# First weights of a fused attention and Mish layer joined from 16-bit halves, and differences moved from GpSimd to VectorE between the two stages

## The chip, the core and the metric

The kernel runs on one core of a Trainium2 chip. The metric is the device time of one execution in microseconds (us); the kernel before took 827.08 us (median of 3 runs, 826.86 to 828.69). The engines are TensorE (PE in the rows; PEld is its weight load), VectorE (DVE), ScalarE (ACT), GpSimd (POOL) and the queue engine SyncE (SP), which issues most transfers.

## What is computed

An attention with queries averaged in pairs, then a two-layer feed-forward block with the Mish function:

```python
q_pool = q.reshape(B, H, S // 2, 2, D).mean(axis=3)            # B, H, S, D = 4, 8, 1152, 64
scores = np.matmul(q_pool, k.transpose(0, 1, 3, 2)) / sqrt(D)
attn = softmax(scores)                                          # over 1152 keys
x = (attn @ v) laid out as 2304 tokens x 512
h = x @ w_in                                                    # 512 x 2048
out = (h * tanh(softplus(h))) @ w_out                           # 2048 x 512
```

q, k and v are float32; w_in and w_out come as float64 and have to be made float32 on the chip.

## The kernel before

**Attention.** 32 steps, one for each batch, pair of heads and half of the 576 queries. A step `i` has nine chunks `c` of 128 keys for both heads of the pair. In the names of the plan: QK(i, c) is TensorE's scores into PSUM; CP copies them to SBUF on ScalarE; MX and MXF keep running maxima on VectorE; MT, TMAX and MB (TensorE, VectorE, TensorE) bring the maximum over keys to every partition; SUB (VectorE) and EXP (ScalarE) work in four groups of chunks; ADD(i, 0 to 4) sums the exponentials on GpSimd, where ADD(i, 2) is a transfer that GpSimd issues and that adds in flight; PV is the product with v; PVE copies it out; FIN0 sums over partitions on TensorE. The division is done by FLN, FEX, FC, FE, FT, FU, FX on ScalarE and GpSimd, and for the last two steps by LX(i) on VectorE (an addition, a reciprocal, a product). The result is xT, x transposed.

**Feed-forward.** x and the weights go into TensorE as a high part (fp32r) and a rest, three products for each. split_h(u, c) rounds a piece of x (unit u of 256 tokens, quarter c of 512) on ScalarE, and split_l(u, c) takes the difference that is the rest; H_(u, f) is the first layer for a unit and a slice of 128 hidden columns; A_g and A_gh are Mish in full and rounded; D_gl is their difference on VectorE; O_(u, f) is the second layer, and EV takes it out of PSUM, for the first block on ScalarE. split_l runs on GpSimd, but for units 5 to 8 in quarters 2 and 3 on VectorE.

**Weights.** 32 pieces of 128 x 512; load_w(n) is the transfer of the raw 64-bit numbers, conv(n, m) the conversion: m = 0 rescales the high word on ScalarE, m = 1, 2 and 3 are three VectorE instructions that shift the exponent into place, put in the sign, and put in three bits of the low word; m = 4 rounds the high part on ScalarE, and m = 5 takes the rest by a difference on GpSimd. Pieces 0 to 3 are converted in steps 0 to 4 of the attention (m = 0 into PSUM there), pieces 4 to 8 in the border between the stages.

**What sets the order.** Each engine runs its instructions in program order, and waits on semaphores. The program order is a sort by planned times in units of a step: FILL lists the first steps one by one, STEP gives each later step, END overrides the last steps (NS = 32), TAIL lists the border with the first units of the feed-forward, FLOW the rest.

Of the kernel before, what the change touches and what calls it, by code (L numbers as in the profile page):

```python
# [22 lines left out]
def tile_pooled_attention_then_mish_ffn(ctx: ExitStack, tc: tile.TileContext, q, k, v, moe_w_in, moe_w_out, out):  # L23
# [43 lines left out]
    if True:  # L67
# [352 lines left out]
        FILL = [  # L420
            (-0.891, load_q, 0, 0),
            (-0.802, load_k, 0, (0, 2)),
            (-0.762, load_k, 0, (2, 5)),
            (-0.703, load_k, 0, (5, 9)),
            (-0.643, QH, 0),
            (-0.624, load_w, 0),
            (-0.602, QK, 0, 0),
            (-0.506, QK, 0, 1),
            (-0.486, CP, 0, 0),
            (-0.466, load_q, 0, 1),  # L430
            (-0.427, QK, 0, 2),
            (-0.407, CP, 0, 1),
            (-0.377, load_w, 1),
            (-0.351, MX, 0, 1),
            (-0.348, QK, 0, 3),
            (-0.328, CP, 0, 2),
            (-0.286, conv, 0, 0),
            (-0.269, QK, 0, 4),
            (-0.253, MX, 0, 3),
            (-0.219, load_k, 1),  # L440
            (-0.218, QH, 1),
            (-0.209, QK, 0, 5),
            (-0.192, MX, 0, 4),
            (-0.187, CP, 0, 3),
            (-0.138, MX, 0, 5),
            (-0.131, QK, 0, 6),
            (-0.084, conv, 0, 1),
            (-0.073, CP, 0, 5),
            (-0.070, QK, 0, 7),
            (-0.041, load_q, 1),  # L450
            (-0.035, MX, 0, 6),
            (-0.016, QK, 1, 0),
            (0.019, MX, 0, 7),
            (0.030, CP, 0, 6),
            (0.073, conv, 0, 2),
            (0.084, CP, 0, 7),
            (0.087, QK, 0, 8),
            (0.137, load_v, 0),
            (0.137, conv, 0, 3),
            (0.154, CP, 0, 8),  # L460
            (0.197, conv, 1, 0),
            (0.210, MX, 0, 8),
            (0.236, CP, 1, 0),
            (0.264, conv, 1, 1),
            (0.279, conv, 0, 4),
            (0.293, QK, 1, 1),
            (0.295, QP, 1),
            (0.313, MXF, 0),
            (0.315, load_w, 2),
            (0.367, MX, 1, 1),  # L470
            (0.379, MT, 0),
            (0.414, conv, 0, 5),
            (0.421, conv, 1, 2),
            (0.427, QK, 1, 2),
            (0.432, CP, 1, 1),
            (0.470, TMAX, 0),
            (0.487, CP, 1, 2),
            (0.489, QK, 1, 3),
            (0.530, conv, 1, 3),
            (0.543, QK, 1, 4),  # L480
            (0.578, MX, 1, 3),
            (0.591, MB, 0),
            (0.594, load_w, 3),
            (0.632, MX, 1, 4),
            (0.644, CP, 1, 3),
            (0.686, conv, 2, 0),
            (0.686, SUB, 0, 1),
            (0.700, QK, 1, 5),
            (0.725, CP, 1, 4),
            (0.752, load_q, 2),  # L490
            (0.768, CP, 1, 5),
            (0.782, QK, 1, 6),
            (0.789, SUB, 0, 0),
            (0.810, EXP, 0, 1),
            (0.892, MX, 1, 5),
            (0.902, EXP, 0, 0),
            (0.946, SUB, 0, 2),
            (0.958, QK, 1, 7),
            (0.989, CP, 1, 6),
            (1.008, ADD, 0, 0),  # L500
            (1.014, PV, 0, 0),
            (1.031, CP, 1, 7),
            (1.049, MX, 1, 6),
# [4 lines left out]
            (1.157, SUB, 0, 3),
            (1.169, QK, 1, 8),
            (1.225, PV, 0, 2),  # L510
            (1.228, ADD, 0, 1),
            (1.237, CP, 1, 8),
            (1.238, load_k, 2),
            (1.268, PV, 0, 1),
            (1.279, CP, 2, 0),
            (1.308, MX, 1, 8),
            (1.335, QK, 2, 1),
            (1.362, conv, 2, 1),
            (1.391, PV, 0, 5),
            (1.403, CP, 2, 1),  # L520
            (1.411, MXF, 1),
            (1.416, load_v, 1),
            (1.435, PV, 0, 4),
            (1.446, EXP, 0, 3),
            (1.465, MX, 2, 1),
            (1.482, MT, 1),
            (1.519, conv, 2, 2),
            (1.531, QK, 2, 2),
            (1.568, TMAX, 1),
            (1.570, QK, 2, 3),  # L530
            (1.590, ADD, 0, 2),
            (1.590, CP, 2, 2),
            (1.627, MX, 2, 3),
            (1.632, conv, 1, 4),
            (1.639, MB, 1),
            (1.674, QK, 2, 4),
            (1.690, SUB, 1, 0),
            (1.691, conv, 1, 5),
            (1.693, CP, 2, 3),
            (1.721, PV, 0, 6),  # L540
            (1.735, CP, 2, 4),
            (1.765, PV, 0, 7),
            (1.793, MX, 2, 4),
            (1.804, EXP, 1, 0),
            (1.812, QK, 2, 5),
            (1.847, SUB, 1, 1),
            (1.860, QK, 2, 6),
            (1.890, CP, 2, 5),
            (1.916, PV, 0, 8),
            (1.933, CP, 2, 6),  # L550
            (1.950, MX, 2, 5),
            (1.975, EXP, 1, 1),
            (2.004, MX, 2, 6),
            (2.016, QK, 2, 7),
            (2.058, SUB, 1, 2),
            (2.070, QK, 2, 8),
            (2.081, ADD, 1, 0),
            (2.084, CP, 2, 7),
            (2.126, PVE, 0),
            (2.150, CP, 2, 8),  # L560
            (2.161, MX, 2, 7),
            (2.163, PV, 1, 3),
            (2.215, MX, 2, 8),
            (2.227, QK, 3, 0),
            (2.269, conv, 2, 3),
            (2.283, PV, 1, 0),
            (2.301, ADD, 0, 3),
            (2.318, MXF, 2),
# [1000 lines left out]
```

## Time and profile before

| | |
|---|---|
| profiled execution | 827.53 us, span 825.5 us |
| median of 3 runs | 827.08 us |
| TensorE busy | 802.4 us, 97% of the span |
| VectorE, ScalarE, GpSimd busy | 566.4, 507.2 and 400.9 us |
| granted TensorE clock, mean | 0.99 |
| attention | up to about 419 us, a step 12.3 us |

A row of the timeline has the start in us, the length, the engine, the line, the operation, out<-in with shapes, how many instructions are merged, and in brackets the idle time of the engine before it with what ended it. Busy shares are means over stages with different limits, so the stages have to be read one by one.

### The profile page before, as it was taken

The page shows a single profiled execution, that of the slowest core. Times are in us where ns is not written, and L with a number is a line of the kernel's source. Part 1 is how long each engine was busy: PE and PEld are TensorE (multiplying, and loading weights), DVE is VectorE, ACT ScalarE, POOL GpSimd, SP SyncE. Part 2 cuts the span into 40 slices and gives each one's busy share as a digit, 9 for nine tenths or more (in the row PEclk, how much of TensorE's full clock was granted, in tenths as well). Part 3 has the DMA queues.
Part 4 walks back from the last instruction along what each step waited for, and adds up shares of the span by engine and source line. Part 5 has one row for each costly group of instructions (what it writes and reads, how often), then busy time and mean ns, then how long its engine had stood idle before and what let it go on. Part 6 is the DMA issues. An engine that isn't in the chain of part 4 may idle for free.

```text
span 825.5 us, 12804 instructions
## 1 busy us (share of the span) xinstructions
PE 802.4 (97%) x4979; PEld 543.1 (66%) x4979; DVE 566.4 (69%) x690; ACT 507.2 (61%) x864; POOL 400.9 (49%) x332
## 2 busy tenths in 40 slices
PE   7899999999999999999998999999999999999997
PEld 4354554554555555554577888888888888888886
DVE  6999999999999999999947334545654433432222
ACT  5799999999999999998956622232333233212211
POOL 2479998898898898897985101110120111100000
PEclk9999999999999999999998999999999999999999
DMA  6446467556557656555422101111120111001111
GB/s 236 138 131 146 120 152 173 138 135 152 126 142 173 144 174 145 130 123 116 87 44 77 52 26 51 52 52 42 60 77 26 52 51 52 1 26 51 52 45 57
DMA packets 21515, 78.93 MB, mean 96 GB/s; under 512 B 2128, under 2 KB 6992, under 8 KB 21456
## 3 DMA queue, kind: packets, MB, share of 16 engines
q0 software_dynamic: 4608, 28.31, 19.2%
q1 hardware_dynamic: 16848, 49.81, 16.5%
q8 instruction: 39, 0.64, 0.3%
q14 instruction: 20, 0.16, 0.1%
HBM read 45.09 MB, written 4.72 MB: 60 GB/s over the span
## 4 chain that ended last, share of the span: by engine, by line
PE 81%; DVE 5%; POOL 5%; ACT 4%; DMA 3%; issue 2%; DVEq 0%; POOLq 0%; ACTq 0%
PE h L1034 22%; PE s L156 18%; PE pv L238 14%; PE o L1075 10%; DMA acc<-TB 3%; PE Sb L260 2%; POOL acc L230 2%; PE mt L192 2%; DVE rmax L177 1%; DVE TA L215 1%; ACT TA L166 1%; POOL acc L224 1%; PE Mb L209 1%; POOL acc L226 1%; ACT TA L219 1%
## 5 line engine op out<-in xcount | busy, mean ns | idle before, releaser
L156 PE MATMUL s<-qT,kT 64*128 64x288 f32 x1152 | 204.4, 451 | 8.9 <-ACT TA L166 3.5
L1043 ACT ACTIVATE g<-h 128x512 f32<-128x512 f32 (+1 forms) x88 | 45.7, 523 | 251.4 <-PE h L1034 251.4
L1051 DVE TENSOR_TENSOR gl<-g,gh 128x512 fp32r<-128x512 f32 (+1 forms) x88 | 55.9, 638 | 201.9 <-ACT gh L1047 196.6
L156 PEld LDWEIGHTS s<-qT,kT 64*128 64x128 f32 x1152 | 93.0, 187 | 105.9 <-DVE rmax L177 27.0
L418 POOL TENSOR_TENSOR wl<-wt,wh 128x512 fp32r<-128x512 f32 x32 | 44.3, 1385 | 242.9 <-ACT wh L415 189.3
L166 ACT COPY TA<-s 128x576 f32<-128x576 f32 x192 | 117.6, 638 | 25.5 <-PE s L156 16.8
L215 DVE TENSOR_TENSOR TA<-TA,Mb 128x1152 f32<-128x1152 f32 x96 | 129.1, 1349 | 2.0 <-PE Mb L209 0.7
L1034 PE MATMUL h<-xh,wh 128*128 128x512 f32 (+1 forms) x352 | 124.7, 354 | 0.0
L1034 PE MATMUL h<-xl,wh 128*128 128x512 f32 (+1 forms) x352 | 124.1, 353 | 0.1
L1034 PE MATMUL h<-xh,wl 128*128 128x512 f32 (+1 forms) x352 | 124.1, 353 | 0.0
L238 PE MATMUL pv<-TA,vn 128*64 128x288 f32 x768 | 115.5, 421 | 0.4 <-ACT pvs L249 0.4
L219 ACT ACTIVATE TA<-TA 128x1152 f32<-128x1152 f32 x96 | 112.8, 1175 | 2.9 <-DVE TA L215 2.3
L224 POOL TENSOR_TENSOR acc<-TA 128x1152 f32<-128x1152 f32 x32 | 85.0, 2657 | 45.3 <-ACT TA L219 29.8
L230 POOL TENSOR_TENSOR acc<-acc 128x576 f32<-128x576 f32 x64 | 91.2, 1425 | 9.3 <-DMA acc<-TB 7.8
L177 DVE TENSOR_TENSOR rmax<-s,rmax 128x576 f32<-128x576 f32 x128 | 93.7, 752 | 1.3 <-ACT TB L166 0.7
L238 PEld LDWEIGHTS pv<-TA,vn 128*64 128x64 f32 x768 | 47.1, 137 | 47.7 <-issue 10.1
L1034 PEld LDWEIGHTS h<-xh,wh 128*128 128x128 f32 x352 | 66.8, 190 | 10.8 <-issue 0.4
L1034 PEld LDWEIGHTS h<-xl,wh 128*128 128x128 f32 x352 | 66.8, 190 | 10.2 <-DVE xl L1006 0.3
L1034 PEld LDWEIGHTS h<-xh,wl 128*128 128x128 f32 x352 | 66.9, 190 | 9.4
L215 DVE TENSOR_TENSOR TB<-TB,Mb 128x1728 f32<-128x1728 f32 x32 | 62.2, 1945 | 0.0
L166 ACT COPY TB<-s 128x576 f32<-128x576 f32 x96 | 59.4, 651 | 4.2 <-PE s L156 3.3
L238 PE MATMUL pv<-TB,vn 128*64 128x288 f32 x384 | 61.5, 415 | 0.2
(404 smaller groups left out, 1326.8 us busy)
## 6 DMA issues: line engine op xcount, KB each, us to landing
acc<-TB POOLq DMA_DIRECT2D x32, 864.0 KB, 7.2
vn<-in_v_dram SPq DMA_DIRECT2D x16, 576.0 KB, 6.3
kT<-in_k_dram SPq DMA_DIRECT2D x15, 576.0 KB, 5.3
qn<-in_q_dram SPq DMA_DIRECT2D x15, 576.0 KB, 6.3
ri<-in_moe_w_in_dram SPq DMA_DIRECT2D x16, 512.0 KB, 3.3
ro<-in_moe_w_out_dram SPq DMA_DIRECT2D x16, 512.0 KB, 3.3
out_dram<-xT SPq DMA_DIRECT2D x18, 256.0 KB, 2.6
qn<-in_q_dram SPq DMA_DIRECT2D x2, 288.0 KB, 4.5
```

The source lines that it names most:

```text
L156: pe.matmul(s[:, j, 0:HQ], kT[64 * j:64 * j + 64, c], qT[64 * j:64 * j + 64, hf], start=True, stop=True,)
L166: act.copy(T(i, c), ss[i, c])
L177: dve.tensor_tensor(ss[i, c] if c == FOLD else r, ss[i, c], x, ALU.max)
L215: dve.tensor_tensor(x, x, Mbs[i].unsqueeze(1).to_broadcast([P, w, W]), ALU.subtract)
L219: act.activation(x, x, AF.Exp, scale=0.0625)
L224: pool.tensor_tensor(accs[i][:, 0:2], T(i, 0, 2), T(i, 2, 4), ALU.add)
L230: pool.tensor_tensor(accs[i][:, 0], accs[i][:, 0], accs[i][:, n - 2], ALU.add)
L238: pe.matmul(pvs[i][64 * j:64 * j + 64, 0:HQ], vn[:, j, c, :], T(i, c)[:, j], start=(pvn[i] == 1), stop=(pvn[i] == NC),)
L1034: pe.matmul(o, a, b, start=(m == 0), stop=(m == len(seq) - 1))
L1043: act.activation(ch[bu, f], hs[bu, f], AF.Mish)
L1051: dve.tensor_tensor(gl, ch.pop((bu, f)), f32(gs[bu, f][0]), ALU.subtract)
L1075: pe.matmul(os_[bu][t], x, y, start=(first and m == 0), stop=(last and m == 2))
```

## The change

For pieces 0 to 3 the float32 word is put together from 16-bit halves: a ScalarE instruction writes the three low bits as an unsigned 16-bit number into the lower half, a GpSimd instruction writes the sign (0 or 32768) into the upper half, and one VectorE instruction shifts the rescaled exponent and mantissa from PSUM and joins them. In the border, split_l of units 5, 6 and 7 is on VectorE in all quarters, and that of unit 8 on GpSimd; conv(n, 5) is on VectorE for pieces 4 to 8. FILL, END, TAIL and two planned times have new numbers; the set of steps is the same.

```diff
+U16 = mybir.dt.uint16
...
+            if n not in wt:
+                wt[n] = wraw_p.tile([P, DM], F32, tag="wt", name=f"wt{n}")
+            if n < 4 and 0 < m < 4:
+                z = wt[n].bitcast(U16).rearrange("p (m two) -> p m two", two=2)
+                u = x.bitcast(U16)
+                if m == 1:
+                    act.activation(z[:, :, 0], u[:, :, 1], AF.Copy, bias=2.0**-14 - 0.5, scale=2.0**-13)
+                elif m == 2:
+                    pool.tensor_scalar(z[:, :, 1], u[:, :, 3], 32768.0, 32768.0, ALU.is_ge, ALU.mult)
+                else:
+                    w = wt[n].bitcast(I32)
+                    dve.scalar_tensor_tensor(
+                        w, in0=cw[n].bitcast(I32), scalar=3, in1=w, op0=ALU.logical_shift_left, op1=ALU.bitwise_or
+                    )
+                return
             if m == 0:
-                wt[n] = wraw_p.tile([P, DM], F32, tag="wt", name=f"wt{n}")
...
-                pool.tensor_tensor(lo, wt[n], f32(hi), ALU.subtract)
+                (dve if 3 < n < 9 else pool).tensor_tensor(lo, wt[n], f32(hi), ALU.subtract)
...
-            e = dve if u > 4 and c in XD else pool
+            e = dve if 4 < u < 8 and c in XD else pool
...
-        XD, ED = (2, 3), ()
+        XD, ED = (0, 1, 2, 3), ()
...
-            (-0.2644, split_h, 3, 3),
+            (-3.3977, conv, 4, 0),
```

How this moves instructions is shown at three places. First VectorE in step 0, from the maximum of chunk 5 to the TMAX of step 0 (s are scores, rmax the running maxima, cw and wt a piece in work, m the maximum). Before:

```order
L177 TENSOR_TENSOR rmax0_0_153<-s0_5_170,rmax0_0_153 128x576
L400 TENSOR_SCALAR cw0_160<-cw0_160 128x512
L177 TENSOR_TENSOR rmax0_1_173<-s0_6_177,rmax0_1_173 128x576
L177 TENSOR_TENSOR rmax0_0_153<-s0_7_183,rmax0_0_153 128x576
L402 SCALAR_TENSOR_TENSOR cw0_160<-ri0_137,cw0_160 128x512
L406 SCALAR_TENSOR_TENSOR wt0_159<-ri0_137,cw0_160 128x512
L177 TENSOR_TENSOR s0_8_196<-s0_8_196,rmax0_1_173 128x2x288
L400 TENSOR_SCALAR cw1_204<-cw1_204 128x512
L181 TENSOR_TENSOR rmax0_0_153<-s0_8_196,rmax0_0_153 128x576
L177 TENSOR_TENSOR rmax1_0_219<-s1_1_212,TA3_101 128x576
L402 SCALAR_TENSOR_TENSOR cw1_204<-ri1_151,cw1_204 128x512
L198 TENSOR_REDUCE m0_238<-mt0_221 128x5
```

and now:

```order
L178 TENSOR_TENSOR rmax0_0_153<-s0_5_171,rmax0_0_153 128x576
L178 TENSOR_TENSOR rmax0_1_174<-s0_6_179,rmax0_1_174 128x576
L405 SCALAR_TENSOR_TENSOR wt0_159<-cw0_161,wt0_159 128x512
L178 TENSOR_TENSOR rmax0_0_153<-s0_7_185,rmax0_0_153 128x576
L178 TENSOR_TENSOR s0_8_196<-s0_8_196,rmax0_1_174 128x2x288
L182 TENSOR_TENSOR rmax0_0_153<-s0_8_196,rmax0_0_153 128x576
L178 TENSOR_TENSOR rmax1_0_216<-s1_1_204,TA3_101 128x576
L199 TENSOR_REDUCE m0_234<-mt0_220 128x5
```

Of the five conversion instructions in this stretch one is left; piece 1 has none before step 2.

Then GpSimd from the affine select at the start to the transfer ADD(0, 2) (qT is the pair sum of queries, wl the rest of a piece, acc the sum of exponentials). Before:

```order
L133 TENSOR_TENSOR qT0_109<-qn0_131 128x288
L130 TENSOR_TENSOR qT1_166<-qn1_186 128x576
L418 TENSOR_TENSOR wl0_0_210<-wt0_159,wh0_0_209 128x512
L224 TENSOR_TENSOR acc0_287<-TA3_101 128x1152
L226 TENSOR_TENSOR acc0_287<-TA3_101 128x576
L228 DMA acc0_287<-TB3_102 128x1728
```

and now:

```order
L402 TENSOR_SCALAR wt0_159<-ri0_137 128x512
L134 TENSOR_TENSOR qT0_109<-qn0_131 128x288
L131 TENSOR_TENSOR qT1_167<-qn1_188 128x576
L433 TENSOR_TENSOR wl0_0_213<-wt0_159,wh0_0_212 128x512
L225 TENSOR_TENSOR acc0_281<-TA3_101 128x1152
L402 TENSOR_SCALAR wt1_209<-ri1_151 128x512
L227 TENSOR_TENSOR acc0_281<-TA3_101 128x576
L433 TENSOR_TENSOR wl0_1_344<-wt1_209,wh0_1_343 128x512
L402 TENSOR_SCALAR wt3_380<-ro1_339 128x512
L402 TENSOR_SCALAR wt2_332<-ro0_218 128x512
L229 DMA acc0_281<-TB3_102 128x1728
```

The four sign instructions (L402) stand ahead of the second half of the first queries, of ADD(0, 1), and, the last two with one difference, of the transfer.

Last GpSimd in the border, from ADD(31, 3) and ADD(31, 4) on (es, pvs and rs belong to the division of step 29, xl is the rest of x). Before:

```order
L230 TENSOR_TENSOR acc31_4033<-acc31_4033 128x576 x2
L276 TENSOR_TENSOR es29_4050<-es29_4050,rs29_4068 128x288
L1006 TENSOR_TENSOR xl2_3961<-xT_60,xh2_3960 128x256
L291 TENSOR_TENSOR pvs29_3901<-pvs29_3901,rs29_4068 128x288
L295 TENSOR_TENSOR xT_60<-es29_4050,pvs29_3901 128x288
L1006 TENSOR_TENSOR xl2_3961<-xT_60,xh2_3960 128x256 x3
L1006 TENSOR_TENSOR xl3_4249<-xT_60,xh3_4248 128x256
L418 TENSOR_TENSOR wl0_2_4295<-wt4_3985,wh0_2_4294 128x512
L1006 TENSOR_TENSOR xl3_4249<-xT_60,xh3_4248 128x256 x5
L418 TENSOR_TENSOR wl1_2_4363<-wt5_4077,wh1_2_4362 128x512
```

and now:

```order
L231 TENSOR_TENSOR acc31_4035<-acc31_4035 128x576 x2
L277 TENSOR_TENSOR es29_4080<-es29_4080,rs29_3997 128x288
L292 TENSOR_TENSOR pvs29_3906<-pvs29_3906,rs29_3997 128x288
L296 TENSOR_TENSOR xT_60<-es29_4080,pvs29_3906 128x288
L956 TENSOR_TENSOR xl2_3936<-xT_60,xh2_3935 128x256 x3
L956 TENSOR_TENSOR xl3_4239<-xT_60,xh3_4238 128x256
L956 TENSOR_TENSOR xl2_3936<-xT_60,xh2_3935 128x256
L956 TENSOR_TENSOR xl3_4239<-xT_60,xh3_4238 128x256 x3
```

The difference between es and pvs stands later, the differences of weights are gone, and of units 5 to 8 four are left.

## Rows read from the trace of the kernel before

**Rows 1.** Windows: stretch in us, length, busy us and count by engine, clock, DMA.

```profile
10.00:20.00 10.00, 7.54 (x51) 4.11 (x49) 9.30 (x15) 6.34 (x12) 2.76 (x3) 0.84 0.58 209
...
100.00:150.00 50.00, 49.80 (x386) 25.54 (x384) 48.68 (x53) 47.32 (x76) 44.93 (x39) 1.00 0.59 143
...
440.00:445.00 5.00, 3.12 (x10) 2.73 (x11) 5.00 (x8) 1.17 (x3) 3.85 (x4) 0.51 0.31 108
```

**Rows 2.** Waits of TensorE, whole run: us in total, times, the longest.

```profile
PE o L1075 <- DVE gl L1051: 3.9, 1, 3.9
PE s L156 <- ACT TA L166: 3.5, 6, 1.8
PE s L156 <- DVE rmax L177: 2.9, 4, 1.7
```

**Rows 3.** Timeline of the first 45 us, VectorE and TensorE.

```profile
12.89 0.69 DVE L406 SCALAR_TENSOR_TENSOR wt<-ri,cw 128x512 int32<-128x512 int32 x1
...
14.91 0.76 PE L156 MATMUL s<-qT,kT 64*128 64x288 f32 x4 [1.84 <-ACT TA L166]
15.06 0.75 DVE L181 TENSOR_TENSOR rmax<-s,rmax 128x576 f32<-128x576 f32 x1
...
23.54 1.35 DVE L215 TENSOR_TENSOR TA<-TA,Mb 128x1152 f32<-128x1152 f32 x1
...
30.30 0.75 DVE L181 TENSOR_TENSOR rmax<-s,rmax 128x576 f32<-128x576 f32 x1
...
31.39 0.76 PE L192 MATMUL mt<-identr,rmax 64*128 64x64 f32 x10
...
44.39 0.76 PE L192 MATMUL mt<-identr,rmax 64*128 64x64 f32 x10
```

**Rows 4.** Timeline of the first 51 us, ScalarE, GpSimd and the first FIN0.

```profile
8.55 0.64 ACT L396 ACTIVATE cw<-ri 128x512 f32<-128x512 f32 x1 [0.75 <-DMA ri<-in_moe_w_in_dram]
...
9.29 0.80 POOL L133 TENSOR_TENSOR qT<-qn 128x288 f32<-128x288 f32 x1 [7.98 <-DMA qn<-in_q_dram]
...
15.44 1.28 POOL L418 TENSOR_TENSOR wl<-wt,wh 128x512 fp32r<-128x512 f32 x1 [0.23 <-ACT wh L415]
...
33.18 1.01 POOL L228 DMA_DIRECT2D acc<-TB  x1 [4.93 <-ACT TB L219]
...
41.24 1.42 POOL L230 TENSOR_TENSOR acc<-acc 128x576 f32<-128x576 f32 x1
...
50.92 0.70 PE L260 MATMUL Sb<-acc,cst 128*64 128x288 f32 x4
```

**Rows 5.** Timeline of the border.

```profile
426.47 0.70 PE L260 MATMUL Sb<-acc,cst 128*64 128x288 f32 x4 [1.05 <-POOL acc L230]
...
428.07 1.08 ACT L1087 COPY xT<-o 128x512 f32<-128x512 f32 x2
...
432.01 1.33 ACT L1001 CAST xh<-xT 128x256 fp32r<-128x256 f32 x4 [2.55 <-DVE xT L288]
...
432.45 0.42 DVE L1006 TENSOR_TENSOR xl<-xT,xh 128x256 fp32r<-128x256 f32 x1
...
437.75 4.66 POOL L1006 TENSOR_TENSOR xl<-xT,xh 128x256 fp32r<-128x256 f32 x5
...
439.14 1.82 DVE L1006 TENSOR_TENSOR xl<-xT,xh 128x256 fp32r<-128x256 f32 x2
```

**Rows 6.** Chain that ended last, border: start, length, engine, output, line, count.

```profile
427.17 0.53 POOL xl L1006
...
429.15 1.96 DVE rs L287
...
443.95 2.56 PE h L1034 x12
...
450.92 5.65 PE h L1034 x48
456.57 2.72 PE o L1075 x12
```

More of the change, by code (lines that the diff above doesn't have):

```diff
@@ L429, in tile_pooled_attention_then_mish_ffn @@
[L429 to L443, printed above, removed]
@@ L476, in tile_pooled_attention_then_mish_ffn @@
[L476 to L491, printed above, removed]
@@ L508, in tile_pooled_attention_then_mish_ffn @@
[L508 to L523, printed above, removed]
@@ L556, in tile_pooled_attention_then_mish_ffn @@
[L556 to L568, printed above, removed]
-            (2.326, PV, 1, 1),
-            (2.346, CP, 3, 0),
-            (2.372, SUB, 1, 3),
@@ new lines, in tile_pooled_attention_then_mish_ffn @@
+            (0.362, CP, 0, 8),
+            (0.373, load_v, 0),
+            (0.376, QK, 1, 1),
+            (0.418, MX, 0, 8),
+            (0.444, CP, 1, 1),
+            (0.486, conv, 1, 1),
+            (0.488, MXF, 0),
+            (0.530, conv, 0, 4),
+            (0.531, QP, 1),
+            (0.542, MX, 1, 1),
+            (0.551, load_w, 2),
+            (0.554, MT, 0),
+            (0.602, QK, 1, 2),
+            (0.619, TMAX, 0),
+            (0.642, QK, 1, 3),
+            (0.649, conv, 0, 5),
@@ new lines, in tile_pooled_attention_then_mish_ffn @@
+            (1.363, CP, 1, 8),
+            (1.396, QK, 2, 1),
+            (1.401, ADD, 0, 1),
+            (1.428, MX, 1, 8),
+            (1.452, PV, 0, 2),
+            (1.464, CP, 2, 1),
+            (1.495, PV, 0, 4),
+            (1.498, MXF, 1),
+            (1.506, EXP, 0, 3),
+            (1.552, MX, 2, 1),
+            (1.564, MT, 1),
+            (1.606, conv, 1, 3),
+            (1.612, QK, 2, 2),
+            (1.631, conv, 2, 1),
+            (1.652, QK, 2, 3),
+            (1.655, TMAX, 1),
@@ new lines, in tile_pooled_attention_then_mish_ffn @@
+            (1.670, load_w, 3),
+            (1.675, CP, 2, 2),
+            (1.714, MX, 2, 3),
+            (1.717, conv, 1, 4),
+            (1.725, MB, 1),
+            (1.760, QK, 2, 4),
+            (1.777, SUB, 1, 0),
+            (1.778, conv, 1, 5),
+            (1.779, CP, 2, 3),
+            (1.808, PV, 0, 6),
+            (1.822, CP, 2, 4),
+            (1.828, load_q, 2),
+            (1.851, PV, 0, 7),
+            (1.880, MX, 2, 4),
+            (1.890, EXP, 1, 0),
+            (1.899, QK, 2, 5),
@@ new lines, in tile_pooled_attention_then_mish_ffn @@
+            (1.934, SUB, 1, 1),
+            (1.947, QK, 2, 6),
+            (1.977, CP, 2, 5),
+            (1.987, conv, 3, 2),
+            (2.003, PV, 0, 8),
+            (2.006, load_k, 2),
+            (2.019, CP, 2, 6),
+            (2.037, MX, 2, 5),
+            (2.066, PVE, 0),
+            (2.068, conv, 2, 2),
+            (2.090, EXP, 1, 1),
+            (2.091, MX, 2, 6),
+            (2.103, QK, 2, 7),
+            (2.145, SUB, 1, 2),
+            (2.150, ADD, 0, 2),
+            (2.157, QK, 2, 8),
@@ new lines, in tile_pooled_attention_then_mish_ffn @@
+            (2.177, CP, 2, 7),
+            (2.184, load_v, 1),
+            (2.213, PV, 1, 2),
+            (2.225, CP, 2, 8),
+            (2.227, ADD, 1, 0),
+            (2.247, MX, 2, 7),
+            (2.256, PV, 1, 3),
+            (2.267, conv, 2, 0),
+            (2.301, MX, 2, 8),
+            (2.311, EXP, 1, 2),
+            (2.313, QK, 3, 0),
+            (2.356, conv, 2, 3),
+            (2.369, PV, 1, 0),
+            (2.404, MXF, 2),
+            (2.413, PV, 1, 1),
+            (2.415, conv, 3, 0),
@@ new lines, in tile_pooled_attention_then_mish_ffn @@
+            (2.447, QP, 2),
+            (2.458, SUB, 1, 3),
+            (2.459, CP, 3, 0),
+            (2.470, QK, 3, 1),
+            (2.502, conv, 3, 1),
+            (2.526, PV, 1, 4),
+            (2.546, CP, 3, 1),
+            (2.565, ADD, 1, 1),
+            (2.578, QK, 3, 2),
+            (2.610, MX, 3, 1),
+            (2.626, MT, 2),
+            (2.646, CP, 3, 2),
+            (2.664, conv, 3, 3),
+            (2.676, QK, 3, 3),
+            (2.688, EXP, 1, 3),
+            (2.713, TMAX, 2),
@@ new lines, in tile_pooled_attention_then_mish_ffn @@
+            (3.359, MX, 3, 8),
+            (3.381, FLN, 0),
+            (3.393, PV, 2, 3),
+            (3.412, EXP, 2, 2),
+            (3.430, MXF, 3),
+            (3.440, QK, 4, 0),
+            (3.484, SUB, 2, 3),
+            (3.496, QK, 4, 1),
+            (3.499, FEX, 0),
+            (3.518, ADD, 2, 1),
+            (3.526, CP, 4, 0),
+            (3.551, PV, 2, 4),
+            (3.569, CP, 4, 1),
+            (3.603, QK, 4, 2),
+            (3.635, MX, 4, 1),
+            (3.637, ADD, 1, 3),
```

1188 lines of the change are left out of this document (540 added, 648 removed).

## The prediction

> **What bounds the kernel now.** I read the windows first. In the middle of the attention TensorE is busy 49.80 of 50 us and VectorE 48.68 [rows 1]: TensorE sets the pace there, and nothing taken off another engine shortens it. Time can be won only where TensorE stands idle or runs below its full clock, and there are two such places. From 10 to 20 us it is busy 7.54 of 10 us with VectorE at 9.30 and a granted clock of 0.84; from 440 to 445 us it is busy 3.12 of 5 us at 0.51, with VectorE at 5.00 [rows 1]. The waits name who is late: scores wait for the maxima (2.9 us) and for the copies (3.5 us), all in the first steps or at the seam, and one second-layer product waits 3.9 us for a difference of Mish [rows 2]. The start and the border are therefore costed apart.
>
> **The start.** Each of pieces 0 to 3 had three VectorE instructions of 0.69 us [rows 3] and keeps one. That is 8 x 0.69 = 5.5 us less VectorE work in the first 50 us, but only what lies on the chain counts, so I follow the new order with the old durations.
>
> ScalarE gets its first raw weights at 8.55 us, when the transfer lands [rows 4]. From there to the copy of chunk 8 of step 0 the new order has nine instructions (seven copies, the rescaling, the new low bits); at 0.63 us (0.64 [rows 4] less a little overlap) that ends at 14.2 us. The maxima that wait for it (two of 0.75 us) end at 15.7 us; in the trace they end at 15.06 + 0.75 = 15.8 us [rows 3]. Up to here the saving on VectorE is spent: ScalarE now does one conversion more and the first copy of step 1 earlier. Next, one maximum, TMAX, a wait for scores until about 19.2 us, two SUB (1.35 us each [rows 3], less overlap) and two maxima bring the third SUB to 23.4 us, against 23.54 [rows 3]. Then two maxima, the SUB of three chunks (half more elements, some 1.95 us) and one maximum follow without a conversion between them, and MXF(1) starts at 28.85 us against 30.30 [rows 3]. The transposes of step 1 follow at 29.65 us against 31.39: **1.75 us gained**. From those transposes to the next TensorE has 13.0 us (31.39 to 44.39 [rows 3]) with 0.9 us of it idle, and one pair of PV products more is put ahead of the second ones, some 0.5 us. VectorE has as many conversions there as before, then two fewer in step 3. I take **2.1 us** for the start; it is kept afterwards, since the steps that follow are full. The bounds are 0.1 us (only what is won up to the third SUB) and 4 us (that, the 0.9 us and part of the lost clock).
>
> The new ScalarE instruction has 128 x 512 elements as the rescaling has: 0.64 us [rows 4], four times. ScalarE has 3.7 us free of 10 there (6.34 busy [rows 1]), so beyond the nine above it costs nothing; if 16-bit stores took twice as long, the first would move the 14.2 us by 0.6.
>
> The new GpSimd instruction has no row. Its neighbours are a two-input sum of 288 elements at 0.80 us and a two-input difference of 512 at 1.28 us [rows 4]. I take 1.28, with 0.5 and 4 us as ends. What it holds up: the first starts at 8.6 us, when the weights land, and ahead of QH(1), 0.80 us, which ends at 10.7 us; QK(1, 0) needs that at 11.75 us. The cover is 1 us. The last two and ADD(0, 1) stand ahead of the transfer ADD(0, 2): its issue goes from 33.18 us [rows 4] to 34.0 + 2 x 1.28 = 36.6 us. Issue to the first following addition took 41.24 - 33.18 = 8.06 us [rows 4], and two additions of 1.42 us follow, so the sum is ready at 47.5 us. TensorE comes to FIN0(0) at 50.92 - 2.1 = 48.8 us [rows 4]. The cover is 1.3 us, which is used up when one sign instruction takes 1.9 us.
>
> The Trainium skill, GPSIMD Engine Reference, Engine selection, advises VectorE for elementwise work and puts one-input instructions on GpSimd at roughly line rate; its Performance pitfalls give about 1.9 cycles an element for strides up to 8 bytes, which for 512 elements at 1.2 GHz would be an estimate of 0.81 us. With that the cover holds and the sum stays; the advice speaks against the step all the same. No row here shows such an instruction.
>
> The transfer load_w(3) now waits in SyncE's queue for the sign of piece 1 (about 28 us) with load_q(2), load_k(2) and load_v(1) behind it. Their first users run after 40 us, so I cost that at nothing; 3 us later and QP(2) on GpSimd would slip.
>
> **The border.** FIN0(31) waits 1.05 us for ADD(31, 4), at 426.47 us [rows 5]; that chain runs over the transfer and does not change. After it GpSimd did a division step, a difference (0.53 us of the chain, with 0.12 us of issue behind it) and another division step, and LX(31) had to wait for that; its reciprocal starts at 429.15 us [rows 6]. The difference now stands later, so LX(31) ends at 431.3 us in place of 432.0: 0.65 us.
>
> ScalarE waited 2.55 us for that and then rounds four pieces in 1.33 us [rows 5], 0.33 each. In the old order the wait that follows is for the difference gl of unit 2 (the 3.9 us [rows 2]): it stands behind conversions and differences of x on VectorE that run at 0.91 us each (1.82 for two) while GpSimd does five in 4.66 us, though the same difference took 0.42 us when GpSimd was idle [rows 5]. The clock then falls to its lower level of 1.2 GHz: the next H_ takes 2.56 us, while later four take 5.65, 1.41 each [rows 6].
>
> In the new order, on the clock of the trace: after 431.3 us VectorE has three conversions (at 0.69 [rows 3], 2.1 us) and the difference for O_(2, 0), ready at 433.8 us. TensorE gets there after O_(1, 0), H_(3, 0), O_(1, 1), H_(3, 1) (1.36 and 1.41 us [rows 6]) at 432.9 us and needs the difference two products later: a wait of 0.4 us. The difference of unit 2 that was late is ready at 435 us and needed at 437.5. H_(5, 0) needs the last rest of unit 5. ScalarE has 18 instructions before it (nine roundings at 0.33 and two EV at 0.54 [rows 5]; six Mish, which have the elements of a rounding and read PSUM, put at 0.36; a weight put at the 0.64 of the rescaling [rows 4]): 6.9 us, to 438.2 us. Three differences of 0.42 follow, and 1.0 us for two rests of unit 8 that GpSimd does beside them: 440.5 us. H_(5, 0), O_(3, 0), H_(5, 1), O_(3, 1) take it to 446.1 us. ScalarE's next 17 instructions take 7.4 us, to 445.6, so the last rest of unit 6 is there at 446.0: H_(6, 0) starts at 446.3 us with a little slack for the issue. Four H_ of 1.41 bring O_(4, 0) to 452.0 us against 456.57 [rows 6]: **4.6 us gained**, made of the idle time, the 0.65 us and the clock. The bounds are 0.65 us (the wait forms again one product later) and 7.5 us (all idle time and clock from 426 us on, FIN0's 1.05 us among it).
>
> The weights' differences that came to VectorE (twice the elements of the 0.42 us rows, so 0.7 us) run beside a full TensorE after 450 us and cost nothing there.
>
> **The sum.** The profiled execution took 827.53 us, 2.0 us outside its span and 0.45 us above the median. 827.53 - 2.1 - 4.6 = 820.8 us, my forecast.
>
> **The rivals.**
>
> *VectorE becomes the bound of the border.* Until H_(6, 0) it has nine conversions at no more than 0.69, fifteen differences at 0.42 and two of weights at 0.7: 13.9 us from 431.3, to 445.2 us, which fits. If the 0.91 us belonged to the place and not to GpSimd's work beside it, the differences would take 13.7 us, the weights' 3.6, the conversions still 6.2: 23.5 us, to 454.8 us, where the trace has H_(6, 0) at 450.92 [rows 6]. That is 3.9 us later, less the start's 2.1: 829.3 us, slower. It turns slower than before when VectorE's work there passes 21.7 us. The 0.42 us beside an idle GpSimd speaks against it.
>
> *The sign instruction is slow.* With p us for one, FIN0(0) comes at 44.9 + 2p. At p = 4 that is 52.9 us, 2.0 us later than before: 827.53 + 2.0 - 4.6 = 824.9 us.
>
> *The start gives nothing*, because ScalarE's nine instructions set it as far as the steady state: 827.53 - 4.6 = 822.9 us. The first 15 us, where only 0.1 us is won, speak for it.
>
> *The wait re-forms behind ScalarE* at O_(2, 0) or H_(5, 0), and only the 0.65 us stay in the border: 824.8 us.
>
> *More than forecast*: 4 us at the start and 6.5 in the border, 817.0 us.
>
> **How the numbers follow.** Forecast 0.60 (819 to 823), VectorE bound 0.09, slow sign 0.06, start nothing 0.10, re-formed wait 0.09, more 0.06. A measurement can tell about 0.2%, 1.65 us, from no change, so faster means below 825.43 us. Faster: 0.60 + 0.10 + 0.06, and 0.09 of the two cases near 825: 0.85. Same: the other 0.06 of those. Slower: 0.09. The range from 817.8 to 825.5 leaves out the slower case, half of the one with more and some of those near 825, 0.18 in all.
>
> **What would show it.** Start: the second set of transposes near 29.7 us and the third near 42.3; sign instructions at 0.8 to 1.3 us; FIN0(0) without a wait for GpSimd. Border: LX(31) ending 0.65 us closer to FIN0(31), differences of x on VectorE at 0.42 us, no wait of some 4 us for gl, and a granted clock near 1.00 from 440 to 450 us. I am wrong if the transposes come at 31 us or later, if the late wait stands before H_(5, 0) or H_(6, 0) with over 2 us, or if VectorE's differences stay at 0.9 us.

## The result

The changed kernel takes 818.57 us (median of four runs, 816.64 to 818.81) against 827.88 us (826.86 to 828.89): 9.3 us less, a ratio of 0.9882 with the 95% interval 0.9861 to 0.9904. Forecast were 820.8 us and a range from 817.8 to 825.5. The profiled execution took 818.65 us, 816.7 us of it its span, 8.8 us shorter than the 825.5 us of before.

The first view is again the windows (stretch, length, busy us and count of PE, PEld, DVE, ACT and POOL, then granted clock, share of DMA, GB/s), for the stretches of [rows 1]:

```profile
10.00:20.00 10.00, 7.89 (x55) 4.49 (x55) 7.68 (x11) 8.03 (x15) 4.29 (x4) 0.83 0.53 198
100.00:150.00 50.00, 50.00 (x390) 25.83 (x388) 49.04 (x54) 47.46 (x76) 44.72 (x37) 1.00 0.60 145
440.00:445.00 5.00, 5.00 (x39) 4.77 (x38) 4.97 (x13) 2.83 (x8) 3.78 (x1) 1.00 0.21 81
```

From 10 to 20 us VectorE's busy time falls from 9.30 to 7.68 us, yet TensorE's clock is no better (0.83). From 440 to 445 us TensorE is busy all 5 us and at full clock, where it had 3.12 us at 0.51. The waits of TensorE over the whole run, in the form of [rows 2]:

```profile
PE s L157 <- ACT TA L167: 1.9, 5, 0.7
PE s L157 <- DVE rmax L178: 1.8, 3, 0.7
...
PE mt L193 <- DVE rmax L182: 1.6, 2, 1.4
...
PE o L1025 <- DVE gl L1001: 0.6, 2, 0.3
PE h L984 <- DVE xl L956: 0.5, 1, 0.5
```

The 3.9 us behind gl have become 0.6, and the waits for copies and maxima have shrunk from 3.5 and 2.9 to 1.9 and 1.8; a wait of 1.4 us ahead of the first transposes is new. Next, TensorE's timeline at the places of [rows 3 to 5] (start, length, engine, line, operation, in brackets the idle time ahead):

```profile
28.40 0.76 PE L193 MATMUL mt<-identr,rmax 64*128 64x64 f32 x10
...
423.02 0.70 PE L261 MATMUL Sb<-acc,cst 128*64 128x288 f32 x4
```

and the chain that ended last (start, length, engine and output, line), as in [rows 6]:

```profile
424.85 1.96 DVE rs L288
...
442.50 5.65 PE h L984 x48
448.15 2.72 PE o L1025 x12
```

The transposes of step 1 come 3.0 us earlier (31.39 before), the last FIN0 3.45 us earlier and without its 1.05 us of waiting, the reciprocal of LX(31) 4.3 us (429.15), and H_(6, 0) 8.4 us (450.92). From H_(6, 0) to the end of the span it is 374.6 us before and 374.2 after, so nearly all the gain lies ahead of it.

Where it comes from shows when the same two stretches of work are cut out of both traces by windows: from 8 us to the first FIN0, and from the transposes of step 31 to H_(6, 0). Before:

```profile
404.41:450.92 46.51, 41.32 (x273) 33.21 (x274) 29.23 (x38) 30.63 (x74) 33.83 (x34) 0.93 0.29 73
...
8.00:50.92 42.92, 36.42 (x250) 18.07 (x250) 41.13 (x51) 32.67 (x47) 18.86 (x13) 0.92 0.47 148
```

and after:

```profile
401.59:442.50 40.91, 39.40 (x273) 31.21 (x274) 31.32 (x45) 28.84 (x70) 30.66 (x29) 1.00 0.34 83
...
8.00:47.74 39.74, 34.16 (x246) 17.09 (x246) 36.38 (x43) 34.13 (x50) 26.82 (x17) 0.96 0.50 166
```

The border is 5.6 us shorter: TensorE stands idle 3.7 us less (5.19 to 1.51 us) and is busy 1.9 us less with the same 273 matmuls. The start is 3.2 us shorter: 0.9 us less idle and 2.3 us less busy, with 250 and 246 matmuls on record (four products with v fewer; a row of four takes 0.71 us). Work that takes less time at the same count is the clock: 0.93 to 1.00 in the border, 0.92 to 0.96 in the start. So in this pair of traces about 3.5 of the 8.8 us are TensorE's clock, 1.9 in the border and some 1.6 in the start; the prediction had counted it inside the border's sum alone. Between the two stretches, from the first FIN0 to the transposes of step 31, the changed kernel takes 0.4 us more (353.85 against 353.49 us). Cut finer, the low level of 1.2 GHz (0.50) stands in before's trace from about 16.9 to 20.3, from 23.7 to 27.1 and from 440.0 to 446.5 us; in after's from 16.2 to 20.0 us and never again.

### The profile page after: what moved, and what is told of

Same layout as the page of the kernel before. It is cut to its first block, busy times and chain, and to the rows that moved or that the text cites. A ratio compares the mean times of both kernels' runs of the same rounds, so it can differ in the third digit from the quotient of the medians.

```text
span 816.7 us, 12779 instructions
## 1 busy us (share of the span) xinstructions
PE 798.1 (98%) x4979; PEld 540.1 (66%) x4979; DVE 564.5 (69%) x691; ACT 508.4 (62%) x868; POOL 402.8 (49%) x327
## 4 chain that ended last, share of the span: by engine, by line
PE 80%; POOL 7%; ACT 4%; DVE 4%; DMA 3%; issue 2%; SPq 0%; DVEq 0%; ACTq 0%; POOLq 0%
PE h L984 23%; PE s L157 17%; PE pv L239 14%; PE o L1025 10%; DMA acc<-TB 2%; POOL acc L231 2%; PE Sb L261 2%; PE mt L193 1%; POOL acc L225 1%; ACT TA L167 1%; PE Mb L210 1%; DVE rmax L178 1%; POOL acc L227 1%; ACT TA L220 1%; DMA ri<-in_moe_w_in_dram 1%
## 5 line engine op out<-in xcount | busy, mean ns | idle before, releaser
L157 PEld LDWEIGHTS s<-qT,kT 64*128 64x128 f32 x1152 | 92.6, 187 | 100.8 <-DVE rmax L178 27.1
L433 POOL TENSOR_TENSOR wl<-wt,wh 128x512 fp32r<-128x512 f32 x27 | 36.3, 1344 | 241.8 <-ACT wh L430 191.8
L225 POOL TENSOR_TENSOR acc<-TA 128x1152 f32<-128x1152 f32 x32 | 85.6, 2675 | 36.1 <-ACT TA L220 23.7
L984 PEld LDWEIGHTS h<-xh,wh 128*128 128x128 f32 x352 | 66.2, 188 | 10.7 <-issue 0.4
```

What stands on the lines that cost most here:

```text
L157: pe.matmul(s[:, j, 0:HQ], kT[64 * j:64 * j + 64, c], qT[64 * j:64 * j + 64, hf], start=True, stop=True,)
L225: pool.tensor_tensor(accs[i][:, 0:2], T(i, 0, 2), T(i, 2, 4), ALU.add)
L984: pe.matmul(o, a, b, start=(m == 0), stop=(m == len(seq) - 1))
```

## The experiments

The theory at this point: two separate gains, about 3 us in the start and 5.7 in the border, which add up; in the border the work that was moved to VectorE carries it, as the prediction had it. The rivals: the border's gain is only its earlier arrival; the border's new order carries it, not the engines; the gain is in truth the clock. Medians and intervals (ratio to the kernel before, beside each on the same chip):

| kernel | median us | runs | ratio, 95% |
|---|---|---|---|
| new start alone | 824.00 | 5 | 0.9944 to 0.9968 |
| new border alone | 822.25 | 6 | 0.9913 to 0.9938 |
| changed kernel, border on the old engines | 818.31 | 4 | 0.9873 to 0.9898 |
| before, border on the new engines | 823.03 | 6 | 0.9934 to 0.9961 |
| before, TensorE kept busy in the border | 825.67 | 11 | 0.9968 to 0.9990 |
| before, TensorE kept busy in the start | 824.01 | 8 | 0.9943 to 0.9971 |
| changed, TensorE kept busy in the start | 817.37 | 4 | 0.9862 to 0.9900 |
| changed, old conversion | 821.95 | 5 | 0.9919 to 0.9953 |
| changed, sign twice | 824.20 | 12 | 0.9947 to 0.9977 |
| changed, one difference moved back | 819.53 | 6 | 0.9876 to 0.9925 |
| changed, again | 818.81 | 6 | 0.9872 to 0.9916 |
| changed, TensorE kept busy in the start, again | 816.69 | 6 | 0.9851 to 0.9898 |

The kernel before had medians of 827.76 to 827.97 us beside them.

**The start alone, the border alone.** In the first the changed kernel gets back before's END, TAIL, planned times and border engines; in the second the kernel before gets those of the changed one.

```diff
-                (dve if 3 < n < 9 else pool).tensor_tensor(lo, wt[n], f32(hi), ALU.subtract)
+                pool.tensor_tensor(lo, wt[n], f32(hi), ALU.subtract)
...
-        XD, ED = (0, 1, 2, 3), ()
+        XD, ED = (2, 3), ()
...
-            (-3.3977, conv, 4, 0),
+            (-0.2644, split_h, 3, 3),
...
```

> The new start alone: first weights joined from 16-bit halves and the new order up to the border; in the border the order and the engines of the kernel before. Theory (two separate gains, about 2.9 us at the start and about 5.8 in the border): 825.0 us, between 824.4 and 825.6, and everything in the border 2.8 to 3.2 us earlier than before, with the same distances there as before (H_(6,0) to the end of the span, the wait of the last normalising sum for GpSimd about 1 us). Rival A (the border waits for something that the start does not move, such as the weights' loads, and gives the shift back): 827.4 to 828.2. Rival B (what ended the border late was only its late arrival; the border's edit does little): 820 to 822.

> The new border alone (its order and its engines), with the start and the body of the kernel before. Theory: 827.9 - 5.8 = 822.1 us, between 821.4 and 822.8, so that the two parts add up to the whole (2.9 + 5.8 = 8.7 of 9.3 measured). If the wait of the last normalising sum for GpSimd (1.05 us before) went with the new order of the border, it is gone here too; if it went only because the body arrives earlier, about 1 us of it stays and the time is 822.8 to 823.3. Rival B (border edit does little): 826.5 to 828.

Measured: 824.00 and 822.25 us, 3.8 and 5.5 us under the kernel before. (The first lies 0.4 us below the range given for it.) Together that is 9.3 us, the whole. Both gains are real and they add up; the border's is no matter of arrival. In the second kernel the last FIN0 comes 21.43 us after the transposes of step 31 (405.37 to 426.80 us) and no longer waits; in the kernel before and with the start alone it is 22.06 us, 1.05 and 1.07 us of it waiting. So that wait went with the border's new order.

**Order or engines.** The changed kernel with the differences back on before's engines, and the kernel before with the engines alone changed:

```diff
-            e = dve if 4 < u < 8 and c in XD else pool
+            e = dve if u > 4 and c in XD else pool
...
-        XD, ED = (0, 1, 2, 3), ()
+        XD, ED = (2, 3), ()
```

> The changed kernel with its new order everywhere, but the differences in the border back on the engines of before (those of x of two column groups and of all weights on GpSimd). Theory E (the engines carry the border's gain: without GpSimd beside them the two-input instructions of VectorE are half as long and g's low part is there in time): most of the 5.8 us is lost, 822.5 to 825 us, with the waits of PE for g's low part back (2 us and more together) and a lower granted clock about 440 us. Theory O (the new order carries it): 818.3 to 820.0 us. In between, about 821, both have a share.

> The kernel before with only the engines changed in the border (the differences of x of all column groups and those of the weights of units 4 to 8 on VectorE), its order of instructions as it was. Theory E (engines carry the gain): 827.9 - 3 to 5 = 823 to 825 us. Theory O (order carries it; in the old order the differences stand on VectorE ahead of what PE waits for): 827 to 830 us, with PE's waits for VectorE in the border longer than before.

Measured: 818.31 us and 823.03 us. The order alone gives all of it, and the prediction's reason falls: the engines are not needed. By themselves they give 4.75 us by the median. In the trace 3.3 us of that are the border's (from the transposes of step 31 to H_(6, 0) 43.25 us in place of 46.51), and 1.5 us come from a start with one stretch of half clock less, though its instructions there are before's. The border's window and TensorE's waits from 405 us on, in the kernel before with the new engines:

```profile
402.92:446.17 43.25, 39.02 (x273) 31.22 (x274) 29.23 (x45) 30.72 (x74) 28.88 (x29) 1.00 0.31 74
...
PE o L1075 <- DVE gl L1051: 1.5, 1, 1.5
PE h L1034 <- POOL xl L1006: 1.4, 1, 1.4
PE Sb L260 <- POOL acc L230: 1.0, 1, 1.0
```

So the engines alone do not remove the waits: one of 3.9 us becomes two of 1.5 and 1.4, and FIN0(31) waits as before. TensorE stands idle 1.0 us less; the other 2.3 us are work done faster (39.02 against 41.32 us for 273 matmuls), at a clock of 1.00 in place of 0.93. Order and engines are no two shares that add up: either shortens the wait for gl so far that the clock stays up. In the kernel with the old engines, VectorE's timeline of the border still shows slow rows beside GpSimd:

```profile
434.59 0.95 DVE L956 TENSOR_TENSOR xl<-xT,xh 128x256 fp32r<-128x256 f32 x1
435.47 1.53 DVE L415 TENSOR_SCALAR wt<-wt 128x512 int32<-128x512 int32 x1
437.04 1.11 DVE L417 SCALAR_TENSOR_TENSOR wt<-ri,wt 128x512 int32<-128x512 int32 x1
```

while TensorE's waits in the border (from 405 us on) are small:

```profile
PE h L984 <- DVE xl L956: 0.7, 1, 0.7
PE o L1025 <- DVE gl L1001: 0.3, 1, 0.3
```

A difference of 256 elements at 0.95 us in place of 0.42 costs nothing if what TensorE needs next stands ahead of it. The Trainium skill, SBUF — State Buffer, Who interferes with whom, says that a VectorE instruction with two SBUF inputs contends with a GpSimd instruction that reads SBUF; the 0.95 and 0.42 us agree, but in this kernel the price was the place in the queue.

**The clock in the border.** In the kernel before, 15 matmuls whose result is thrown away stand in the 3.9 us in which O_(2, 1) waits for gl. They write into the PSUM buffer of the next H_.

```diff
                     pe.matmul(os_[bu][t], x, y, start=(first and m == 0), stop=(last and m == 2))
+                    if (bu, f, t, m) == (2, 1, 0, 1):
+                        spare_h.append(pools["psH"].tile([P, 512], F32, tag="h", name="hbusy"))
+                        for _ in range(NBUSY):
+                            pe.matmul(spare_h[0], x, y, start=True, stop=True)
```

> The kernel before, with 15 additional matmuls (128x128 by 128x512, result thrown away) in the 3.9 us in which PE waits for the low part of g in the border; nothing else changed, and the wait itself stays. Theory C (a part of that wait's price is the clock, granted at half from 440.0 to 446.5 us after it): the granted clock stays 1.00 there, the 4.6 us of matmuls from 441.9 to 446.5 take half as long, 825.5 us, between 825.0 and 826.2. Theory W (the price is the wait alone): 827.3 to 828.3 us whatever the clock does.

Measured: 825.67 us, 2.1 us less, interval 0.9968 to 0.9990. TensorE's timeline shows the wait filled and just as long:

```profile
438.32 3.57 PE L1080 MATMUL hbusy<-wl,gh 128*128 128x512 f32 x15
442.39 0.50 PE L1076 MATMUL o<-wh,gl 128*128 128x512 f32 x1 [0.49 <-DVE gl L1052]
```

and the granted clock from 440 to 445 us is 1.00 (0.51 before). The three matmuls behind the first one after the wait take 0.39 to 0.40 us each, where they took 0.63, and from the transposes of step 31 to H_(6, 0) it is 44.31 us in place of 46.51. So of the border's 5.5 us about 2 are the clock that fell during the wait, as the windows had it (1.9 us).

**The clock in the start.** Transposes of the identity into a PSUM buffer that is free until the first PV, behind some scores. In the kernel before 48 of them, in the changed one 34:

```diff
             ss[i, c] = s[:, :, 0:HQ]
+            for n in range(BUSY.get((i, c), 0)):
+                if not busy:
+                    busy.append(ps1.tile([P, 4, P], F32R, tag="pv", name="busy"))
+                pe.transpose(busy[0][:, n % 4], identr, identr)
```

> The kernel before with 48 additional 128x128 transposes of the identity (result thrown away) in PE's waits between 7.6 and 23.7 us; nothing else changed. Theory C (in the start, too, half of what the change gains is the clock: two stretches at half clock, 16.9 to 20.3 and 23.7 to 27.1 us, of which the changed kernel has one): both are gone, MT(1) comes 1.5 to 3 us earlier than at 31.39, and the time is 824.8 to 826.3 us. Theory W (the waits for VectorE set the pace there, not the clock): 827.2 to 828.3 us.

> The changed kernel with 34 additional 128x128 transposes of the identity (result thrown away) in PE's waits between 7.5 and 15.5 us; nothing else changed. Theory C (the one stretch of half clock that is left, 16.2 to 20.4 us, follows those waits and holds 3.8 us of matmuls): it is gone, MT(1) comes 0.8 to 1.9 us earlier than at 28.40, and the time is 816.7 to 817.8 us. Theory W (VectorE and ScalarE set the pace there, and PE's clock does not matter): 818.2 to 819.0 us. If the transposes hold up the first matmuls: 819 to 820 us.

Measured: 824.01 us, 3.75 us under the kernel before and as much as the whole new start gives; and 817.37 us. In both traces the granted clock is 1.00 throughout the first 52 us. The windows of the changed kernel with the transposes, to be held against its 0.83 above:

```profile
10.00:20.00 10.00, 9.08 (x78) 5.77 (x76) 8.18 (x11) 8.44 (x15) 4.12 (x4) 1.00 0.55 198
```

The kernel before with its transposes comes to the first FIN0 at 49.88 us, the changed one with its own at 47.37: at equal clock the new start is ahead by 2.5 us, of which up to 0.9 us is a first set of transposes that the extra work itself delays (16.72 us in place of 15.86).

The totals agree with theory C, or go beyond it, but the transposes of step 1 moved less than it expected. They come 1.0 us earlier in the kernel before (30.36 us; 1.5 to 3 were expected) and 0.4 us earlier in the changed one (28.00; 0.8 to 1.9 were expected):

```profile
30.36 0.76 PE L197 MATMUL mt<-identr,rmax 64*128 64x64 f32 x10
...
28.00 0.76 PE L198 MATMUL mt<-identr,rmax 64*128 64x64 f32 x10
```

The rest of what the totals gain stands later. From the first FIN0 to the transposes of step 31 the two kernels take 1.0 and 1.6 us less than without the idle transposes (352.53 against 353.49 us, 352.23 against 353.85), at full clock with and without. In this stretch the changed kernel without them has

```profile
PE Sb L261 <- POOL acc L231: 1.8, 2, 1.0
...
288.23 1.42 POOL L231 TENSOR_TENSOR acc<-acc 128x576 f32<-128x576 f32 x1 [1.79 <-DMA acc<-TB]
...
294.71 0.70 PE L261 MATMUL Sb<-acc,cst 128*64 128x288 f32 x4 [0.85 <-POOL acc L231]
```

that is, GpSimd's sum waits 1.79 us for the transfer that adds, and FIN0 waits for that sum; the same happens about 50 us later. In the three traces with idle transposes in the start GpSimd waits 0.3 to 0.9 us at these places and FIN0 does not wait; the other eleven traces have 0.5 to 2.1 us of FIN0's wait between 52 and 405 us. Why the transfer is there sooner is not shown, so these totals are no measure of the clock.

What the clock costs in the start is seen better where the same start has, from one execution to another, a different number of stretches at half clock. The kernel before has a granted clock of 0.84 from 8 to 30 us and the changed one 0.92; the kernel before with the new engines in the border, and the changed kernel with one difference moved back (below), have it the other way round:

```profile
8.00:30.00 22.00, 16.27 (x109) 8.06 (x105) 21.04 (x28) 16.10 (x25) 7.46 (x5) 0.92 0.58 208
49.45 0.70 PE L260 MATMUL Sb<-acc,cst 128*64 128x288 f32 x4
...
8.00:30.00 22.00, 17.41 (x109) 8.65 (x105) 17.82 (x22) 16.88 (x26) 11.64 (x7) 0.84 0.37 137
49.44 0.70 PE L261 MATMUL Sb<-acc,cst 128*64 128x288 f32 x4
```

| start | stretches at half clock | first FIN0, us |
|---|---|---|
| before's | two (three traces) | 50.89 to 50.95 |
| before's | one (one trace) | 49.45 |
| new | two (one trace) | 49.44 |
| new | one (four traces) | 47.74 to 48.03 |

One stretch costs about 1.5 us there, and with equally many stretches the new start is ahead by 1.4 to 1.7 us. The runs of the kernel before beside these experiments point the same way on the whole time, border included: three with a mean clock of 0.998 took 823.4 to 825.6 us, nine with 0.988 took 827.9 to 830.3 us.

To see whether the 817.37 us are a better kernel, the changed kernel stood beside it, both once more on one chip:

> The changed kernel unaltered, on the same chip as the runs beside it: 818.2 to 818.9 us.

> The changed kernel with the 34 transposes in PE's waits between 7.5 and 15.5 us, beside the changed kernel on the same chip. If the stretch at half clock behind those waits costs time: 0.8 to 1.5 us below the changed kernel, 817.0 to 817.8 us, and granted clock 1.00 from 10 to 30 us. If what showed 817.4 us was chance: within 0.4 us of the changed kernel.

Measured: 818.81 us (818.04 to 819.44) and 816.69 us (816.25 to 819.09). Five of the six runs lie below all six of the changed kernel, one inside. The median difference is 2.1 us; the intervals against the kernel before overlap. Most likely this version beats the changed kernel by 1 to 2 us. In the traces 0.6 us of that lie ahead of the first FIN0 (48.00 to 47.39 us) and 1.7 us between it and step 31, where the changed kernel's FIN0 waits 2.0 us for GpSimd and this one does not; that the clock does all of it is not shown.

**The conversion, apart from the order.** The changed kernel with before's three VectorE instructions for pieces 0 to 3, in the new places but for seven of them, which are moved to where the old chain has its inputs:

```diff
-            if n < 4 and 0 < m < 4:
...
-                return
...
-            (-0.071, conv, 0, 2),
+            (0.150, conv, 0, 2),
...
```

> The changed kernel with its new order everywhere, but the first four weights converted as before: three instructions on VectorE (0.41 + 0.69 + 0.69 us) in place of one on VectorE (0.69), one on ScalarE and one on GpSimd. Theory J (the start's gain is VectorE's freed time, 1.1 us for each of the two pieces ahead of MT(1)): MT(1) 1.1 to 2.2 us later than at 28.40, total 820.0 to 821.5 us. Theory O (the new order of the start carries it): 818.2 to 819.3 us.

Measured: 821.95 us, 3.1 to 3.4 us more than the changed kernel, some more than its theory had. One reason is that the theory took 0.41 us for the first of the three instructions, its time in the border; here it takes 0.69 us as the others do, so a piece has 1.4 us more on VectorE and not 1.1:

```profile
27.72 0.69 DVE L402 TENSOR_SCALAR cw<-cw 128x512 int32<-128x512 int32 x1
```

TensorE's timeline has the transposes of step 1 1.5 us later, and beyond them waits for VectorE that the changed kernel does not have:

```profile
29.93 0.76 PE L193 MATMUL mt<-identr,rmax 64*128 64x64 f32 x10 [0.73 <-DVE rmax L182]
...
42.92 0.76 PE L157 MATMUL s<-qT,kT 64*128 64x288 f32 x4 [0.74 <-DVE rmax L182]
```

The new order of the start needs the light join: without it, it gains little over before's (the new border with before's start took 822.25 us), though it was not fitted to the old instructions. The run does not tell what the join would give in before's order; that was not tried.

**More work on GpSimd.** The sign instruction of pieces 2 and 3 is given twice, the second time with the same result:

```diff
-                    pool.tensor_scalar(z[:, :, 1], u[:, :, 3], 32768.0, 32768.0, ALU.is_ge, ALU.mult)
+                    for _ in range(2 if n > 1 else 1):
+                        pool.tensor_scalar(z[:, :, 1], u[:, :, 3], 32768.0, 32768.0, ALU.is_ge, ALU.mult)
```

> The changed kernel with the sign instruction on GpSimd (2.1 us each) given twice for the third and fourth weight, so 4.2 us more on GpSimd ahead of the sums of step 0; nothing else changed. Theory S (GpSimd's sums ahead of the first normalising sum, FIN0(0), have 0.57 us to spare behind the four sign instructions): FIN0(0) waits 3 to 3.7 us, and the total is 821.3 to 822.4 us. Theory N (GpSimd has room enough there): 818.2 to 819.0 us. A part of the wait can come back later, where GpSimd's sums are ahead of PE: 819.5 to 821.

Measured: 824.20 us, 5.4 us more, beyond what either theory had, and the wait does not stand at FIN0(0). VectorE's and TensorE's timelines:

```profile
41.22 0.69 DVE L406 SCALAR_TENSOR_TENSOR wt<-cw,wt 128x512 int32<-128x512 int32 x1 [2.89 <-POOL wt L403]
41.82 0.75 DVE L182 TENSOR_TENSOR rmax<-s,rmax 128x576 f32<-128x576 f32 x1
```

```profile
42.72 1.33 PE L157 MATMUL s<-qT,kT 64*128 64x288 f32 x4 [3.13 <-DVE rmax L182]
```

The join on VectorE needs the sign from GpSimd. It waits 2.89 us, the maximum MXF(2) stands behind it in VectorE's queue, TensorE waits 3.13 us for that, and then the clock falls: the windows give 0.66 from 40 to 50 us. In the changed kernel the same join starts with no wait:

```profile
38.11 0.68 DVE L405 SCALAR_TENSOR_TENSOR wt<-cw,wt 128x512 int32<-128x512 int32 x1
```

GpSimd ends its signs there at 36.66 us, so this join has a cover of 1.45 us. FIN0(0) has 0.57 us (its sums end at 47.17 us, it starts at 47.74). With the doubled sign the sums end at 52.79 us, 5.6 us later, and TensorE, already held up, comes to FIN0(0) at 52.92 us: both paths are late by about as much, and the run does not part their prices. It does show that there are two.

**One difference moved back.** The difference of x of unit 4, second column group, ahead of the last division of step 29 again:

```diff
-            (1.5477, split_l, 4, 1),
+            (1.4000, split_l, 4, 1),
```

> The changed kernel with one instruction moved back: the difference of x for unit 4, second column group, on GpSimd ahead of the last steps of block 29 again, as in the kernel before. Theory (the prediction's first border term): the last normalising step of the last block 0.65 us later, up to 0.86, and the total 819.1 to 819.6 us. Rival (the wait it moves is covered by other work): 818.2 to 818.9 us.

Measured: 819.53 us beside 818.81, 0.7 us more, but the intervals overlap, so the total alone does not decide. VectorE's and TensorE's timelines do:

```profile
424.91 0.70 PE L261 MATMUL Sb<-acc,cst 128*64 128x288 f32 x4
```

```profile
427.45 1.96 DVE L288 RECIPROCAL rs<-rs 128x288 f32<-128x288 f32 x1
```

From the last FIN0 to the reciprocal of LX(31) it is 2.54 us, in the changed kernel 1.83 and before 2.68. This one instruction is 0.71 us there, as the prediction had it (0.65); 0.44 us of it reach H_(6, 0), 41.35 us after the transposes of step 31 in place of 40.91.

## Why the prediction came out as it did

The time was in the range and on the right side, 2.2 us below the forecast: in the traces the start gave 1.1 us more than its term and the border 1.0. By its own steps:

- **Start, 2.1 us.** Measured 3.0 us at the transposes of step 1 (forecast 1.75) and 3.2 us at FIN0(0). VectorE's part was near the mark, a little below it: with equally many stretches at half clock the new start is 1.4 to 1.7 us ahead. The rest, about 1.5 us, is that the trace before has a second stretch of half clock, 23.7 to 27.1 us, and the trace after has not. The term left the clock out, because it was worked out from VectorE's and ScalarE's durations with matmuls as in the trace; the lost clock stood only inside its upper bound of 4 us. And since either start has one stretch in some executions and two in others, how far this part belongs to the change is not shown by two traces.
- **ScalarE's new instruction.** 0.77 us at its first use against the 0.64 taken; ScalarE had room, and the waits for its copies shrank.

```profile
9.81 0.77 ACT L400 ACTIVATE wt<-ri 128x512 uint16<-128x512 uint16 x1
```

- **GpSimd's sign instruction.** No row had it; 1.28 us was taken, between 0.5 and 4, and it took 2.1 us, as GpSimd's timeline shows:

```profile
8.76 2.14 POOL L402 TENSOR_SCALAR wt<-ri 128x512 uint16<-128x512 uint16 x1 [7.45 <-DMA ri<-in_moe_w_in_dram]
...
32.48 4.18 POOL L402 TENSOR_SCALAR wt<-ro 128x512 uint16<-128x512 uint16 x2
```

  By the prediction's formula FIN0(0) would have waited from 1.9 us on; it did not, because the transfer was issued at 36.58 us, the very time forecast. That was luck: the last two signs took 1.6 us longer than taken and began 1.5 us earlier than the prediction had them. The first sign brought QH(1) to 11.64 us in place of 10.7, which used up the cover named for it, and TensorE shows no wait for it. The estimate of 0.81 us from the Trainium skill, GPSIMD Engine Reference, Performance pitfalls, does not agree: measured is 2.6 times that, and the measurement decides. What the working missed is another place: the join waits for ScalarE and GpSimd, and the prediction named what stands behind the sign on GpSimd but not what stands behind the join on VectorE. The doubled sign shows TensorE's wait there.
- **Border, 4.6 us.** Measured 5.6 us from the transposes of step 31 to H_(6, 0). The count of the new order was good: from the end of LX(31), 427.6 us, H_(6, 0) comes 14.9 us later, forecast 15.0. What was left out lies ahead of it: the wait of FIN0(31) was called unchanged and went (0.63 us net), and LX(31) came 0.85 us closer to FIN0 in place of 0.65.
- **The reason given for the border** was wrong in part. The prediction laid the vanished wait to VectorE's differences at 0.42 us in place of 0.91. In the changed kernel they are that fast where GpSimd stands idle beside them, but the run on the old engines has the same total with rows of 0.95 us. The new order, which has gl and the rests in the order in which TensorE asks for them, is enough; the engines alone are worth 3.3 of the 5.6 us, 2.3 of it by the clock. For the same reason the rival "VectorE becomes the bound" fell by more than its own condition: there the rows stayed slow, and it did not come.
- **The clock in the border** was named rightly as part of the sum, and the filled wait sizes it: about 2 us.

What stays open: why the same start, before's or the new one, has one stretch of half clock in one profile and two in another; why FIN0's waits for GpSimd late in the attention are gone with idle transposes in the start; what the join alone, in before's order, is worth; and which of the two late paths sets the price of a slower sign.

## What to carry to other kernels

Price a wait of TensorE twice, once for its idle time and once for the clock that may fall behind it; where a wait can't be removed, matmuls without use in it can hold the clock at the price of a few lines (2.1 us for the 3.9 us wait of the border). Follow such a gain through the trace before crediting it: in the start, only 0.4 to 1.0 us of 1.2 to 3.75 us stood where the clock had risen. When an instruction collects from several engines, look at what is queued behind it on its own engine: a slow helper shows there too. And when a change moves work to another engine and reorders it at once, test the order alone before believing in the engine.

## What the runs showed of the hardware

A GpSimd instruction with one 16-bit input read every 8 bytes (128 x 512, compare and multiply) took 2.1 us, longer than its two-input float32 difference of the same count (1.28 us). A ScalarE instruction from and to 16-bit halves took 0.77 us against 0.64 for float32. TensorE's granted clock went to 0.50 (1.2 GHz) for 3 to 7 us during or soon after waits of 0.4 to 3.9 us, and with extra matmuls in these waits it did not; kernels whose start has the same instructions showed one such stretch there or two, some 1.5 us apart in time, with before's start and with the new one. A VectorE difference of 128 x 256 took 0.42 us beside an idle GpSimd and 0.91 to 0.96 us beside GpSimd's differences. In eleven of fourteen traces TensorE waited 0.5 to 2.1 us late in the attention for sums that wait for an accumulating transfer.
